# Joins of a block's half-words behind the sixth first-layer product, and token numbers behind a step's last copy

## The chip, the core and the metric

The kernel runs on one core of one Trainium2 chip. The metric is the device time of one execution in microseconds (us). A core has several engines that run side by side, each with its own queue of instructions, worked off in order: TensorE (PE in the profile; PEld is its weight load), VectorE (DVE), ScalarE (ACT), GpSimd (POOL) and SyncE (SP), which here only issues transfers (DMA). An instruction that waits holds up whatever stands behind it in its own queue.

## The reference

Two parts follow one another. First, attention over channels, for each of 4 batches with 5056 rows and 256 channels:

```python
qn = q / (np.linalg.norm(q, axis=1, keepdims=True) + 1e-06)
kn = k / (np.linalg.norm(k, axis=1, keepdims=True) + 1e-06)
s = kn.transpose(0, 2, 1) @ qn / tau      # 256 x 256 per batch
a = softmax(s)                            # over the last axis
x = v @ a                                 # 5056 x 256 per batch
```

Then a mixture of 8 experts over all 20224 tokens, in which each token goes to one expert:

```python
logits = x @ w_gate + modality_bias[modality_id]
e = argmax(logits);  gate = softmax(logits)[e]
out = gate * (relu(x @ w1[e]) @ w2[e])    # 256 -> 1024 -> 256
```

All of it is in 32-bit floating point.

## The kernel before

**Number format.** A 32-bit matrix product is written as three products of a faster format: each operand is split into a high part (a cast, on ACT) and a low part (the rest, a subtraction on DVE), and high by high, high by low and low by high are added up in PSUM. The splits of activations and weights are much of the work of ACT and DVE.

**Steps.** The tokens are handled in 40 steps of 512 (10 for each batch). A step loads its rows of v, transposes them, splits them (`vh`, `vl`), multiplies them by the batch's softmaxed matrix and the gate's weights (`av`, L574), and copies the result xp from PSUM into a tile x: for each of 4 groups of 128 tokens, ACT copies the high half-words (L580) and DVE the low ones. `route` (from L584) works out the softmax and the expert of each token (ACT's exponential ex is L592, the one-hot choice oh L600); `place` counts with small matmuls on PE (rp, L625 to L627) which row each token gets, writes the gate's denominator and the token's number into the two last columns of x (L646, on ACT), and sends the rows (`send`, POOL's indirect DMA, L469) to a buffer xs in DRAM that is sorted by expert. Three buffers serve x, two more at the start.

**The next batch's matrix.** Beside the steps of a batch run the pieces for the next batch's k-by-q matrix: loads of q and k, casts of them (L312), squares, and products g (L357). For the second batch, whose pieces run beside the first batch's steps, the casts and squares on ACT and DVE are ordered behind what an earlier step left in `routed`; its entry for ACT is the copy of the token numbers, L646.

**Blocks.** As soon as an expert has 512 rows, a block of them is chosen (`pick`) and put through the two layers; there are 40 blocks (the last two have 384 rows). Blocks 37 to 39 are chosen when all the steps are done and are called tail blocks. A block's pieces are:

- its loads on SP: the expert's weights, and its rows from xs by a transposing DMA into the tile Tx (L748, two buffers), which holds high and low half-words in separate planes;
- `tr_x`: for each of two halves `join` puts the half-words together to a 32-bit tile xt (high ones by ACT at L512, low ones by DVE at L513), which is then cast to xh (ACT, L808) and subtracted to xl (DVE, L809). xt shares three buffers with v's joins and with squares; xh and xl have two buffers each;
- `split_w(0)` to `split_w(3)`: casts of a quarter of both weights (ACT, L789) and their low parts (DVE, L796);
- `m1(j)`, eight first-layer products (PE, L823), each into one of two PSUM buffers hp, and its two evictions: hh = relu (ACT, L826) and hl, the low part (DVE, L827);
- `m2(j)`, the second-layer products (PE, L843), two products behind the first layer; the last two of a block run after the first product or two of the next block;
- `finish` and the stores (POOL, L469), each ordered behind a relu of the next block.

**What sets the order.** `block_stream` (L929) lists a block's pieces and puts those of the next block in between: `split_w(0)`, `tr_x` and `split_w(1)` at positions 7, 10 and 13 of the list, that is ahead of the fifth product, behind the sixth and ahead of the eighth; at 7, 14 and 15, behind the eighth product, if the next block is a tail block. The list begins with the block's first product, one second-layer product of the block before, and the second product; in a tail block the second-layer product comes first. The streams of a step, of a block and of the next batch are then interleaved. A planner decides from this program, from buffers and from its own simulated times in what order each engine's queue gets its instructions: an instruction that it takes to be ready early may come far ahead of its place in the program. `order` (L455) forbids that for one pair: the instruction doesn't come ahead of the other one. It adds no wait on the chip where both are on one engine.

Of the kernel before, what the change touches and what calls it, by code (L numbers as in the profile page):

```python
# [8 lines left out]
F32 = mybir.dt.float32  # L9
# [26 lines left out]
def kernel(  # L36
# [13 lines left out]
    nc = tc.nc  # L50
    P = 128
    B, N, C = q.shape
    T, D = out.shape
    E, _, FF = w1.shape
    TT = 4
# [5 lines left out]
    NJ = FF // P  # L61
# [40 lines left out]

    const.tile([P, 120], F32, name="filler0")
    ident = const.tile([P, P], F32, name="ident")
# [100 lines left out]
    turn = {}  # L205
# [302 lines left out]

    def join(dst, high, low):

        both = dst.bitcast(U16).rearrange("p (n w) -> p w n", w=2)
        nc.scalar.copy(both[:, 1, :], high)  # L512
        nc.vector.tensor_copy(both[:, 0, :], low)  # L513

    def va_pieces(b, s):
# [4 lines left out]
        st = {}  # L520
# [44 lines left out]
        def av(t):  # L565
# [13 lines left out]
            planes = st["x"][:, t, 0:D].bitcast(U16).rearrange("p (w n) -> p w n", w=2)  # L579
            nc.scalar.copy(planes[:, 0, :], halfwords[:, 1, :])  # L580
            copied[g, t] = nc.vector.tensor_copy(planes[:, 1, :], halfwords[:, 0, :]).ins
# [35 lines left out]
        def place():  # L617
# [22 lines left out]
            with nc.allow_low_precision("row numbers, below 2**24"):  # L640
                numbers = nc.vector.tensor_reduce(pi, pos.rearrange("p e t -> p t e"), AX.X, ALU.add)
            st["pi"] = pi
            routed[g] = [
                ("dve", numbers.ins),
                ("dve", nc.vector.reciprocal(x[:, :, D].bitcast(F32), sm).ins),
                ("act", nc.scalar.copy(x[:, :, D + 1], tokid[:, b, s * TT : (s + 1) * TT]).ins),  # L646
            ]
# [82 lines left out]
    def block_pieces(g, slot, picked, tail):  # L730
# [3 lines left out]
        rows = tt * P  # L734
        beside = {}

        banks = ["y0", "y1"] + (["g"] if slot == NB_MIN - 1 and tt == 3 else [])
# [40 lines left out]
        def split_w(ci):  # L778
            a, c = st["wr"][ci // 2]
            o = ci % 2  # L780
            if slot == 0 and ci == 0:
                p4.tile([P, 64], F32, tag="filler3", name="filler3", bufs=1)
            sa = a[:, :, o * FCH : (o + 1) * FCH]
# [15 lines left out]

        def tr_x():  # L800
            if slot == 0:
# [3 lines left out]
            for h in range(CH):  # L805
                vt = p3.tile([P, STEP], F32, tag="vt", name=f"xt_{slot}_{h}")
                join(vt[:, 0:rows], st["T"][:, 0, h, 0:rows], st["T"][:, 1, h, 0:rows])
                st["turned"] = nc.scalar.copy(xh[:, h, 0:rows], vt[:, 0:rows]).ins  # L808
                nc.vector.tensor_tensor(  # L809
                    xl[:, h, 0:rows], vt[:, 0:rows], xh[:, h, 0:rows].bitcast(F32), ALU.subtract  # L810
                )

        def m1(j):
# [8 lines left out]
            for i, (w, x, h) in enumerate(seq):  # L822
# [3 lines left out]
            relu = nc.scalar.activation(hh[:, 0:rows], hp[:, 0:rows], AF.Relu).ins  # L826
            nc.vector.scalar_tensor_tensor(  # L827
                hl[:, 0:rows], hp[:, 0:rows], 0.0, hh[:, 0:rows].bitcast(F32), ALU.max, ALU.subtract
            )
            st["h"][j] = (hh, hl)  # L830
            for f in beside.get(j, ()):
                f([relu])
# [58 lines left out]
        else:  # L891
# [4 lines left out]
            "slot": slot, "load": prep, "prep": prep2, "tail": tail, "first": lambda: m1(0), "body": body, "last": last,  # L896
            "stores": stores, "beside": beside,
        }
# [30 lines left out]
    def block_stream(blk, nxt):  # L929
# [4 lines left out]
        if nxt is not None:  # L934
            once(nxt, "load")
            done.add((nxt["slot"], "prep"))
            for o, f in reversed(list(zip((7, 14, 15) if nxt["tail"] else (7, 10, 13), nxt["prep"]))):
                body.insert(o, f)
# [4 lines left out]
        if not before:  # L943
            return [blk["first"]] + body
        if blk["tail"]:
            return [before[0], blk["first"], body[0]] + before[1:] + body[1:]
        return [blk["first"], before[0], body[0]] + before[1:] + body[1:]
# [141 lines left out]
```

## Time and profile before

| | us |
|---|---|
| median of 3 runs (lowest, highest) | 1219.19 (1216.51, 1222.01) |
| the profiled execution's own time | 1225.98 |
| its span | 1224.2 |
| PE busy | 1178.0 (96%) |
| DVE busy | 913.3 (75%) |
| ACT busy | 817.7 (67%) |
| POOL busy | 355.0 (29%) |

The profile is of one execution. A group's row reads: line, engine, operation, output <- inputs, count | busy us, mean ns of one | idle time ahead of it and what ended most of that. A timeline row reads: start in us, duration in us, engine, line, operation; in brackets the idle time ahead of it and what ended it. SPq is the issue of a transfer by SP. Matmuls are pipelined, so that the duration of one is longer than the distance to the next. A row of waits reads: engine, output, line <- engine, what was waited for, its line: sum in us, count, longest. PEclk is TensorE's granted clock as a share of full speed, "DMA share" the mean busy share of the core's 16 DMA engines.

### The profile page before, as it was taken

Reading aid. Unit: us, or ns where it says so; the run is one execution under the profiler, and the core shown is the slowest. Engines: PE = TensorE matmul, PEld = TensorE weight load, DVE = VectorE, ACT = ScalarE, POOL = GpSimd, SP = SyncE. Lnnn points to the kernel's source line nnn. Section 1 sums busy time; section 2 is a strip of 40 time slices with the busy share of each in tenths; the row PEclk is TensorE's granted clock in tenths of the full one; section 3 lists DMA queues with packets and bytes.
Section 4 is the critical chain, followed back from the end, with each engine's and each line's share of the span. In section 5 each row is a group of like instructions: output and inputs, shape, how many; then the busy total and the mean of one; then the engine's idle time right before and its main releaser. Section 6 shows DMA issues by size and latency. Waiting matters only on the chain. (4 is left out here: it accounts for less than half of the span.)

```text
span 1224.2 us, 23515 instructions
## 1 busy us (share of the span) xinstructions
PE 1178.0 (96%) x7780; PEld 1071.1 (87%) x7780; DVE 913.3 (75%) x2614; ACT 817.7 (67%) x1659; POOL 355.0 (29%) x345
## 2 busy tenths in 40 slices
PE   8987899999999999999999999999999999988997
PEld 7976799999999999989999999998888988887996
DVE  6787798898778888689887887676767666764552
ACT  6656677787777777588777776666666655544652
POOL 0053142322323222322333332222223322343121
PEclk9997899999999999999999999999999999998998
DMA  8989989499757787479777776647675655545320
GB/s 311 288 230 212 248 236 230 144 241 242 209 164 203 188 214 204 145 205 231 205 201 201 198 191 178 164 142 197 173 189 161 175 152 152 148 124 145 105 87 30
DMA packets 285844, 228.40 MB, mean 187 GB/s; under 512 B 185064, under 2 KB 243944, under 8 KB 285712
## 3 DMA queue, kind: packets, MB, share of 16 engines
q1 hardware_dynamic: 270032, 185.19, 58.2%
q0 software_dynamic: 15680, 41.61, 10.0%
q8 instruction: 63, 1.03, 0.4%
q14 instruction: 69, 0.57, 0.2%
HBM read 128.79 MB, written 43.43 MB: 141 GB/s over the span
## 5 line engine op out<-in xcount | busy, mean ns | idle before, releaser
L843 PE MATMUL y<-w2h,hh 128*128 128x256 f32 x1256 | 356.1, 284 | 0.0
L843 PE MATMUL y<-w2l,hh 128*128 128x256 f32 x1256 | 354.2, 282 | 0.0
L843 PE MATMUL y<-w2h,hl 128*128 128x256 f32 x1256 | 352.6, 281 | 0.1
L469 POOL DMA_INDIRECT xs<-x,pi x160 | 183.5, 1147 | 404.5 <-DVE pr L691 199.8
L469 POOL DMA_INDIRECT out_dram<-yo,gt x158 | 157.7, 998 | 428.3 <-ACT hh L826 251.0
L823 PE MATMUL hp<-xh,w1h 128*128 128x512 f32 (+1 forms) x640 | 254.5, 398 | 12.7 <-DVE hl L827 11.4
L823 PE MATMUL hp<-xh,w1l 128*128 128x512 f32 (+1 forms) x640 | 253.9, 397 | 0.0
L823 PE MATMUL hp<-xl,w1h 128*128 128x512 f32 (+1 forms) x640 | 252.1, 394 | 0.0
L843 PEld LDWEIGHTS y<-w2h,hh 128*128 128x128 f32 x1256 | 238.6, 190 | 12.7 <-issue 4.0
L843 PEld LDWEIGHTS y<-w2l,hh 128*128 128x128 f32 x1256 | 237.9, 189 | 8.0
L827 DVE SCALAR_TENSOR_TENSOR hl<-hp,hh 128x512 fp32r<-128x512 f32 (+1 forms) x320 | 217.1, 679 | 33.8 <-ACT hh L826 32.8
L843 PEld LDWEIGHTS y<-w2h,hl 128*128 128x128 f32 x1256 | 237.9, 189 | 0.3 <-DVE hl L827 0.3
L826 ACT ACTIVATE hh<-hp 128x512 fp32r<-128x512 f32 (+1 forms) x320 | 189.5, 592 | 50.9 <-PE hp L823 47.8
L789 ACT CAST w1h<-w1r 128x512 fp32r<-128x512 f32 x160 | 99.1, 619 | 110.0 <-PE hp L823 93.5
L796 DVE TENSOR_TENSOR w1l<-w1r,w1h 128x512 fp32r<-128x512 f32 x160 | 109.9, 687 | 52.8 <-ACT w1h L789 45.6
L823 PEld LDWEIGHTS hp<-xh,w1h 128*128 128x128 f32 x640 | 121.2, 190 | 29.7 <-DVE hl L827 13.3
L823 PEld LDWEIGHTS hp<-xh,w1l 128*128 128x128 f32 x640 | 121.3, 189 | 27.7
L796 DVE TENSOR_TENSOR w2l<-w2r,w2h 128x512 fp32r<-128x512 f32 x160 | 110.0, 687 | 45.7 <-ACT w2h L789 28.8
L823 PEld LDWEIGHTS hp<-xl,w1h 128*128 128x128 f32 x640 | 121.4, 190 | 15.1 <-DVE xl L809 0.2
L512 ACT COPY xt<-Tx 128x512 uint16<-128x512 uint16 (+1 forms) x80 | 61.7, 775 | 91.0 <-DMA Tx<-xs 87.3
L789 ACT CAST w2h<-w2r 128x512 fp32r<-128x512 f32 x160 | 100.0, 625 | 16.5 <-PE y L843 14.1
L513 DVE COPY xt<-Tx 128x512 uint16<-128x512 uint16 (+1 forms) x80 | 36.1, 460 | 80.5 <-DMA Tx<-xs 80.5
(160 smaller groups left out, 1910.0 us busy)
## 6 DMA issues: line engine op xcount, KB each, us to landing
w1r<-in_moe_w_dram SPq DMA_DIRECT2D x80, 512.0 KB
w2r<-in_moe_w_dram SPq DMA_DIRECT2D x80, 512.0 KB
q<-in_q_dram SPq DMA_DIRECT2D x35, 512.0 KB
k<-in_k_dram SPq DMA_DIRECT2D x35, 512.0 KB
pl<-T SPq DMA_DIRECT2D x120, 128.0 KB
v<-in_v_dram SPq DMA_DIRECT2D x6, 512.0 KB
xs<-x,pi POOLq DMA_INDIRECT x160
out_dram<-yo,gt POOLq DMA_INDIRECT x158
```

The lines of the kernel that those rows point to most:

```text
L469: ins = nc.gpsimd.indirect_dma_start(out=dst, out_offset=bass.IndirectOffsetOnAxis(ap=idx, axis=0), in_=rows, in_offset=None, bounds_check ...
L512: nc.scalar.copy(both[:, 1, :], high)
L513: nc.vector.tensor_copy(both[:, 0, :], low)
L789: ins = nc.scalar.copy(hi, src).ins
L796: nc.vector.tensor_tensor(lo, src, hi.bitcast(F32), ALU.subtract)
L823: nc.tensor.matmul(hp[:, 0:rows], w[:, h, fs], x[:, h, 0:rows], start=i == 0, stop=i == len(seq) - 1)
L826: relu = nc.scalar.activation(hh[:, 0:rows], hp[:, 0:rows], AF.Relu).ins
L827: nc.vector.scalar_tensor_tensor(hl[:, 0:rows], hp[:, 0:rows], 0.0, hh[:, 0:rows].bitcast(F32), ALU.max, ALU.subtract)
L843: ins = nc.tensor.matmul(y, a[:, tsl], w[:, j % 2, :], start=(j == 0 and i == 0 and t % per == 0), stop=(j == NJ - 1 and i == 2), skip_gro ...
```

## The change

1. The joins of a block (both halves, ACT's and DVE's) are ordered behind the evictions of the sixth first-layer product of the block before it: ACT's behind the relu, DVE's behind the low part. The first block's joins stay without such an order.
2. The copy of a step's token numbers is ordered behind the step's last ACT copy of x. As `routed` holds that copy, the second batch's casts and squares that are ordered behind it move along.
3. For tail blocks, the pieces of the next block stand at the same positions as elsewhere (7, 10, 13), and the block's list begins with its own first product as elsewhere.
4. Two tiles that only take up room change in size (120 to 104 and 64 to 72 floats in each partition), which shifts the addresses of the tiles behind them.

```diff
@@ -100,7 +100,7 @@
 
 
 
-    const.tile([P, 120], F32, name="filler0")
+    const.tile([P, 104], F32, name="filler0")
     ident = const.tile([P, P], F32, name="ident")
     make_identity(nc, ident)
     ones = const.tile([P, P], F32, name="ones")
@@ -506,11 +506,11 @@
                 nc.sync.dma_start(out[part * W : (part + 1) * W, w, :, 0:rows], T[w::2, part::2, 0:rows])
         return out
 
-    def join(dst, high, low):
+    def join(dst, high, low, behind=()):
 
         both = dst.bitcast(U16).rearrange("p (n w) -> p w n", w=2)
-        nc.scalar.copy(both[:, 1, :], high)
-        nc.vector.tensor_copy(both[:, 0, :], low)
+        order(nc.scalar.copy(both[:, 1, :], high).ins, behind[:1])
+        order(nc.vector.tensor_copy(both[:, 0, :], low).ins, behind[1:])
 
     def va_pieces(b, s):
         rows = min(STEP, N - s * STEP)
@@ -577,7 +577,7 @@
                 )
             halfwords = xp[:, 0:D].bitcast(U16).rearrange("p (n w) -> p w n", w=2)
             planes = st["x"][:, t, 0:D].bitcast(U16).rearrange("p (w n) -> p w n", w=2)
-            nc.scalar.copy(planes[:, 0, :], halfwords[:, 1, :])
+            st["out"] = nc.scalar.copy(planes[:, 0, :], halfwords[:, 1, :]).ins
             copied[g, t] = nc.vector.tensor_copy(planes[:, 1, :], halfwords[:, 0, :]).ins
             nc.vector.tensor_tensor(st["L"][:, t, :], xp[:, D:DE], bsel[b][:, s * TT + t, :], ALU.add)
 
@@ -640,10 +640,12 @@
             with nc.allow_low_precision("row numbers, below 2**24"):
                 numbers = nc.vector.tensor_reduce(pi, pos.rearrange("p e t -> p t e"), AX.X, ALU.add)
             st["pi"] = pi
+            named = nc.scalar.copy(x[:, :, D + 1], tokid[:, b, s * TT : (s + 1) * TT]).ins
+            order(named, [st["out"]])
             routed[g] = [
                 ("dve", numbers.ins),
                 ("dve", nc.vector.reciprocal(x[:, :, D].bitcast(F32), sm).ins),
-                ("act", nc.scalar.copy(x[:, :, D + 1], tokid[:, b, s * TT : (s + 1) * TT]).ins),
+                ("act", named),
             ]
             if g not in HELD:
                 send()
@@ -733,6 +735,7 @@
         tt = tiles(slot)
         rows = tt * P
         beside = {}
+        evicted = {}
 
         banks = ["y0", "y1"] + (["g"] if slot == NB_MIN - 1 and tt == 3 else [])
         per = -(-tt // len(banks))
@@ -779,7 +782,7 @@
             a, c = st["wr"][ci // 2]
             o = ci % 2
             if slot == 0 and ci == 0:
-                p4.tile([P, 64], F32, tag="filler3", name="filler3", bufs=1)
+                p4.tile([P, 72], F32, tag="filler3", name="filler3", bufs=1)
             sa = a[:, :, o * FCH : (o + 1) * FCH]
             sc = c[:, 2 * o : 2 * o + 2, :]
             res = []
@@ -797,14 +800,14 @@
                 res += [hi, lo]
             st["wc"][ci] = res
 
-        def tr_x():
+        def tr_x(behind=()):
             if slot == 0:
                 p2.tile([P, 24], F32, tag="filler4", name="filler4")
             xh = st["xh"] = p2.tile([P, CH, BLK], F32R, tag="xh", name=f"xh_{slot}")
             xl = st["xl"] = p2.tile([P, CH, BLK], F32R, tag="xl", name=f"xl_{slot}")
             for h in range(CH):
                 vt = p3.tile([P, STEP], F32, tag="vt", name=f"xt_{slot}_{h}")
-                join(vt[:, 0:rows], st["T"][:, 0, h, 0:rows], st["T"][:, 1, h, 0:rows])
+                join(vt[:, 0:rows], st["T"][:, 0, h, 0:rows], st["T"][:, 1, h, 0:rows], behind)
                 st["turned"] = nc.scalar.copy(xh[:, h, 0:rows], vt[:, 0:rows]).ins
                 nc.vector.tensor_tensor(
                     xl[:, h, 0:rows], vt[:, 0:rows], xh[:, h, 0:rows].bitcast(F32), ALU.subtract
@@ -824,10 +827,11 @@
             hh = p3.tile([P, BLK], F32R, tag="hh", name=f"hh_{slot}_{j}")
             hl = p3.tile([P, BLK], F32R, tag="hl", name=f"hl_{slot}_{j}")
             relu = nc.scalar.activation(hh[:, 0:rows], hp[:, 0:rows], AF.Relu).ins
-            nc.vector.scalar_tensor_tensor(
+            low = nc.vector.scalar_tensor_tensor(
                 hl[:, 0:rows], hp[:, 0:rows], 0.0, hh[:, 0:rows].bitcast(F32), ALU.max, ALU.subtract
-            )
+            ).ins
             st["h"][j] = (hh, hl)
+            evicted[j] = [relu, low]
             for f in beside.get(j, ()):
                 f([relu])
 
@@ -894,7 +898,7 @@
         stores = [] if slot >= NB_MIN - 1 else [lambda behind, t=t: store(t, behind) for t in range(tt)]
         return {
             "slot": slot, "load": prep, "prep": prep2, "tail": tail, "first": lambda: m1(0), "body": body, "last": last,
-            "stores": stores, "beside": beside,
+            "stores": stores, "beside": beside, "evicted": evicted,
         }
 
 
@@ -934,7 +938,8 @@
         if nxt is not None:
             once(nxt, "load")
             done.add((nxt["slot"], "prep"))
-            for o, f in reversed(list(zip((7, 14, 15) if nxt["tail"] else (7, 10, 13), nxt["prep"]))):
+            split0, turn, split1 = nxt["prep"]
+            for o, f in reversed(list(zip((7, 10, 13), (split0, lambda: turn(blk["evicted"][NJ - 3]), split1)))):
                 body.insert(o, f)
         before = open_blk[0]["last"] if open_blk[0] is not None else []
         for i, f in enumerate(open_blk[0]["stores"] if before else []):
@@ -942,8 +947,6 @@
         open_blk[0] = blk
         if not before:
             return [blk["first"]] + body
-        if blk["tail"]:
-            return [before[0], blk["first"], body[0]] + before[1:] + body[1:]
         return [blk["first"], before[0], body[0]] + before[1:] + body[1:]
 
     va = [va_pieces(*divmod(g, NS)) for g in range(G)]
```

## The prediction

> **What bounds the kernel now.** I read the page's head and groups first, then what the engines wait for, then busy time by stage.
>
> ```profile
> span 1224.2 us, 23515 instructions
> ...
> L843 PE MATMUL y<-w2h,hh 128*128 128x256 f32 x1256 | 356.1, 284 | 0.0
> ...
> L843 PE MATMUL y<-w2h,hl 128*128 128x256 f32 x1256 | 352.6, 281 | 0.1
> ...
> L789 ACT CAST w1h<-w1r 128x512 fp32r<-128x512 f32 x160 | 99.1, 619 | 110.0 <-PE hp L823 93.5
> ```
>
> The stages, cut at the gaps in TensorE's work; the first column after the stage is its length, the second PE's busy time:
>
> ```profile
> core 0: us, PE busy (x) PEld busy (x) DVE busy (x) ACT busy (x) POOL busy (x), PEclk, DMA share, GB/s
> ...
> 135.00:147.00 12.00, 8.02 (x37) 6.96 (x36) 6.24 (x27) 6.79 (x15) 0.98 (x1) 0.72 1.01 291
> 147.00:830.00 683.00, 681.82 (x4673) 624.35 (x4672) 562.62 (x1547) 508.03 (x1027) 208.78 (x193) 1.00 0.74 197
> 830.00:1075.70 245.70, 239.44 (x1582) 215.64 (x1581) 168.65 (x538) 150.16 (x309) 75.44 (x75) 1.00 0.62 169
> 1075.70:1103.30 27.60, 24.31 (x147) 21.85 (x146) 17.68 (x72) 11.20 (x22) 12.04 (x12) 0.94 0.48 126
> 1103.30:1133.30 30.00, 25.75 (x147) 22.77 (x146) 13.59 (x23) 14.62 (x28) 9.88 (x9) 0.89 0.49 136
> ...
> 1157.10:1179.60 22.50, 22.50 (x146) 20.33 (x145) 11.78 (x21) 11.63 (x23) 3.91 (x4) 1.00 0.38 117
> ```
>
> From 147 to 830 PE idles 683.00 − 681.82 = 1.2 us: that stretch is a queue of matmuls at full clock, and this change takes no matmul away. What can be won lies ahead of 147 and behind 830. The last three rows are blocks 34, 35 and 37, each of the same 146 to 147 matmuls: block 37, with no gap, takes 22.50, the other two 27.60 and 30.00. The waits say what stands behind the gaps; the columns are wait, count and longest:
>
> ```profile
> PE rp L625 <- DVE oh L600: 13.2, 3, 8.9
> PE hp L823 <- DVE hl L827: 11.4, 8, 3.8
> ...
> ACT xt L512 <- DMA Tx<-xs: 87.3, 25, 6.3
> ACT x L646 <- DMA xs<-x,pi: 7.7, 2, 6.7
> ```
>
> PE's 11.4 us are put down to DVE's evictions, but an eviction is 0.7 us of work. ACT stands 87.3 us in 25 waits of the join for a block's transposed rows Tx. What that does, in blocks 34 and 35:
>
> ```profile
> 1087.35 0.76 ACT L512 COPY xt<-Tx 128x512 uint16<-128x512 uint16 x1 [4.36 <-DMA Tx<-xs]
> 1087.99 0.58 ACT L826 ACTIVATE hh<-hp 128x512 fp32r<-128x512 f32 x1
> ...
> 1090.41 0.50 PE L823 MATMUL hp<-xh,w1h 128*128 128x512 f32 x1 [3.29 <-DVE hl L827]
> ...
> 1114.87 0.63 ACT L512 COPY xt<-Tx 128x384 uint16<-128x384 uint16 x1 [3.43 <-DMA Tx<-xs]
> ```
>
> The join stands in ACT's queue (its low half likewise in DVE's) until Tx has landed, the relu of a finished product behind it; both hp buffers stay full, and PE stops. The rows so awaited aren't even needed yet, as a block of the middle shows:
>
> ```profile
> 623.47 0.79 ACT L512 COPY xt<-Tx 128x512 uint16<-128x512 uint16 x1 [2.54 <-DMA Tx<-xs]
> ...
> 607.61 0.39 PE L823 MATMUL hp<-xh,w1h 128*128 128x512 f32 x1
> 636.07 0.39 PE L823 MATMUL hp<-xh,w1h 128*128 128x512 f32 x1
> 636.30 0.39 PE L823 MATMUL hp<-xl,w1h 128*128 128x512 f32 x1
> ...
> 636.79 0.68 DVE L809 TENSOR_TENSOR xl<-xt,xh 128x512 fp32r<-128x512 f32 x1
> ```
>
> Blocks begin 636.07 − 607.61 = 28.46 us apart. The join of 623.47 gets its xl at 636.79, after the block of 636.07 has read its own xl (636.30). So it belongs to the block after that, due near 664.5: joined 41 us ahead.
>
> **Part 1: joins behind the sixth product's evictions.** No instruction is added; the joins move most of a block later, when Tx has long landed, and evictions no longer stand behind the wait. *Tail.* Against block 37, blocks 34 and 35 lose 27.60 + 30.00 − 2 × 22.50 = 12.6 us: PE's idle time 3.29 + 4.25 = 7.5 (27.60 − 24.31 and 30.00 − 25.75), and about 5 of slower matmuls after each gap. The granted clock shows these, and one more stretch that part 2 needs:
>
> ```profile
> 139.30:146.10 6.80, 5.87 (x23) 5.07 (x23) 4.80 (x22) 4.38 (x9) 0.22 (x1) 0.50 1.00 334
> 1091.60:1095.00 3.40, 3.40 (x16) 3.23 (x15) 3.23 (x16) 0.60 (x1) 2.07 (x3) 0.50 0.76 227
> 1115.50:1122.30 6.80, 5.80 (x20) 5.13 (x21) 3.44 (x6) 1.84 (x4) 4.13 (x4) 0.50 0.34 106
> ```
>
> 3.40 and 6.80 us at clock 0.50 lose half of PE's busy time there, 1.7 + 2.9 = 4.6. I take 12; bounds 7.5 and 12.6. The Trainium skill, "TensorE: Matmul & The Clock Gate", section "Part 1: The HAM clock gate", says that the clock falls after a whole idle window of about 3.4 us and needs one busy window to come back; by it each gap would cost half of 3.4, together 3.4 instead of 4.6, and the total would come out 1.2 us later than mine. The rows agree for the first gap (3.40) and not for the second, twice as long.
>
> *830 to 1075.* PE idles 245.70 − 239.44 = 6.3 us. Of the 11.4 us in 8 hp waits above, 3.3 and 3.8 were the tail's; the other six, 4.3 together, are of the same make, nearly all here:
>
> ```profile
> 906.60 0.78 ACT L512 COPY xt<-Tx 128x512 uint16<-128x512 uint16 x1 [4.05 <-DMA Tx<-xs]
> ```
>
> I take these 4; bounds 0 (another queue member stands there instead) and 6.3.
>
> *What the delay costs.* After the sixth product's relu come two joins (0.78 each), two casts (0.62 each, as the weights' of one shape) and the last xl (0.68): 0.59 + 1.56 + 1.24 + 0.68 ≈ 4.1 us if nothing comes between.
>
> ```profile
> 655.65 0.59 ACT L826 ACTIVATE hh<-hp 128x512 fp32r<-128x512 f32 x1
> 664.54 0.39 PE L823 MATMUL hp<-xh,w1h 128*128 128x512 f32 x1
> ...
> 655.65:664.54 8.89, 8.89 (x68) 8.16 (x66) 8.07 (x27) 7.51 (x16) 0.98 (x1) 1.00 0.74 175
> ...
> 1149.20 0.59 ACT L826 ACTIVATE hh<-hp 128x512 fp32r<-128x512 f32 x1
> ...
> 1157.14 0.39 PE L823 MATMUL hp<-xh,w1h 128*128 128x512 f32 x1
> ```
>
> In the middle there are 8.89 us for it, margin 4.7; ACT is already busy for 7.51 of them, some of it casts of weights and of a later block that can wait. At the tail's end 7.94, which the old order there had put one product (a sixteenth of 22.50, 1.4 us) later; margin about 2.4. I take 0; bounds 0 and rival B. Tx has two buffers, so the load of the block after next now waits for these joins on SP; its rows are joined a whole block later, which covers the 6.3 us that a join waited at most. Behind it on SP stand the v transposes and the next weights; that is the cover to watch.
>
> *Tail order.* Turning at the usual place and one first-layer product first: 0, since it changes the order of the same matmuls; with late joins it would cost 1.4.
>
> **Part 2: token numbers behind the step's last copy.** No instruction is added; L646 moves past copies on ACT's queue.
>
> ```profile
> 94.81 0.20 ACT L646 COPY x<-tokid 128x4 int32<-128x4 int32 x1 [6.68 <-DMA xs<-x,pi]
> 98.15 0.18 PE L625 MATMUL rp<-oh,trim 128*128 128x32 bf16 x1 [8.90 <-DVE oh L600]
> 99.85 0.77 ACT L512 COPY xt<-Tx 128x512 uint16<-128x512 uint16 x1
> 107.00 0.73 PE L823 MATMUL hp<-xh,w1h 128*128 128x512 f32 x2 [1.03 <-ACT x L580]
> ...
> 137.46 1.14 ACT L312 CAST qs<-q 128x512 fp32r<-128x512 f32 x2 [4.11 <-DMA q<-in_q_dram]
> ...
> 159.34 0.36 ACT L580 COPY x<-xp 128x256 uint16<-128x256 uint16 x1
> 171.93 1.59 PE L357 MATMUL g<-qs,ks 128*128 128x256 f32 x12
> ```
>
> At 94.81 the copy has held ACT for 6.68 us until scatters of its x buffer were done; the softmax of the step stood behind it, and PE 8.90. With copies ahead of it, these go on. But the first block's rows are only joined at 99.85, after their own transfer, so its first product comes at about 102 at best, 5 us earlier. At 137.46 the q casts, which hang on the same list of routed work, wait for q; they go behind step 7's last copy, 159.34, which frees ACT. Their products run at 171.93, a cover of 12 us. This could save the stage's 12.00 − 8.02 = 4.0 us of idle time and half of PE's 5.87 busy at clock 0.50, 2.9; together with the first, at most 12. At the other end a q wait of 4.11 merely comes elsewhere: −4. The middle of −4 and 12 is 4, and I take it: the first stage is short of transfers too (DMA share 1.01 from 135 to 147), so not the full gain.
>
> **Part 3: fillers.** The addresses of later tiles shift. The nearest rows are the two second-layer groups of equal shape: 356.1 and 352.6 us. I take 0, bounds ±3.5.
>
> **Sum.** 12 + 4 + 4 = 20. The profiled execution takes 1225.98 (the span and 1.8 around it), which is 6.8 above the median of 1219.19; against itself it would come to 1206. If that is waiting for transfers, some of my 20 is missing in the median run; I can't tell, keep 20 there, and get **1199**.
>
> **Rivals.** *A: only the tail gains.* At the start transfers set the pace, and the short gaps of 830 to 1075 reappear at other members of ACT's queue. For: DMA share 1.01, and 8.9 us of rp waits that need q and the scatters anyway. Against: the gaps have one and the same releaser. 1219.2 − 12 = 1207.
> *B: slower, the joins come too late.* The first product of each block waits for its last xl. It decides once more than 4.7 us of other ACT work comes between relu and last cast: one split of the weights is four casts of 0.62, 2.5 us, and two of them 5.0. For: ACT has 7.51 busy in 8.89. Against: three of these are the joins and casts that move. At 1.5 us in each of 683 / 28.46 = 24 blocks it costs 36: 1199 + 36 = 1235.
> *C: the wait moves.* The join still waits for Tx, since Tx's own load now stands behind later joins on SP, with the v transposes behind it; evictions seven and eight stand behind it as before. For: ACT's 87.3 us of these waits show that loads land late against the queue. Against: loads now have a block's time. Gains and new gaps cancel: 1217.
> *That the order is not what it says*: it only forbids earlier joins, so the planner may put them later still; that is B's mechanism.
>
> **From this the numbers.** Forecast 0.60 (its own range 1188 to 1208, 12.6 + 6.3 + 12 saved at one end, the tail's 7.5 and half of the other 8 at the other), A 0.18, C 0.10, B 0.12. A measurement here tells about 0.5% from no change, 6.1 us: faster is below 1213.1, slower above 1225.3. The forecast and A are faster, 0.78 and a little of C, 0.79; C gives 0.10 for the same; B 0.11 with its near end within the bound. Range 1187 to 1217: it takes in A and C and leaves B and the far tails out.
>
> **What would show it.** Right: blocks 34 and 35 last 22.5 to 23.5 us, no clock of 0.50 after 1080, and the joins' 87.3 us of waiting fall below 20. Rows 830 to 1075 show PE idle below 2.5 us. The wait of L646 for scatters falls below 2 and the first block's first product comes before 104. The middle stage remains 683 within 3. Wrong: waits of first-layer products for xl (B), of joins for Tx (C), or rp waits that stay near 13 (A).

## The result and the profile after

The changed kernel takes 1203.80 us (median of 4 runs, 1203.36 to 1206.59) against 1218.18 (median of 4, 1216.51 to 1222.01): ratio 0.988, 95% interval 0.985 to 0.991, or 14.4 us. The forecast was 1199, or 20 us. The two profiled executions lie further apart, 1225.98 and 1203.36, 22.6 us, because the one before was 7.8 us above its median and the one after is 0.4 below.

The head and one matmul group of the page of the changed kernel (its lines stand 3 or 4 further down than before: L826 was L823, L847 was L843, L811 was L808, L829 was L826, L751 was L748, and the token copy L646 is now L643):

```profile
span 1201.6 us, 23565 instructions
...
PE 1170.8 (97%) x7780; PEld 1069.3 (89%) x7780; DVE 914.6 (76%) x2614; ACT 808.5 (67%) x1659; POOL 381.2 (32%) x345
...
L826 PE MATMUL hp<-xh,w1h 128*128 128x512 f32 (+1 forms) x640 | 251.2, 393 | 0.6 <-ACT xh L811 0.6
```

What PE and then ACT wait for (sum, count, longest):

```profile
PE rp L625 <- DVE sm L614: 6.3, 4, 3.4
PE g L357 <- ACT ks L312: 4.5, 1, 4.5
PE g L357 <- DMA k<-in_k_dram: 4.4, 1, 4.4
PE rp L626 <- DVE run L611: 3.0, 2, 2.4
...
PE hp L826 <- ACT xh L811: 0.6, 1, 0.6
...
ACT x L580 <- DMA xs<-x,pi: 9.3, 6, 1.6
...
ACT acc L336 <- DMA k<-in_k_dram: 5.5, 2, 4.5
...
ACT xt L512 <- DMA Tx<-xs: 5.2, 1, 5.2
```

The joins' 87.3 us of waiting are 5.2, and PE's 11.4 us of hp waits behind DVE's evictions are gone. So is ACT's wait in the token copy; copies of x now wait for scatters instead (9.3 us in 6 waits, the longest 1.6). PE's waits are for routing (rp) and for the next batch's products (g). By stage, cut at first-layer products of blocks 0, 2, 12, 14, 24, 34 and 37:

```profile
core 0: us, PE busy (x) PEld busy (x) DVE busy (x) ACT busy (x) POOL busy (x), PEclk, DMA share, GB/s
107.38:158.87 51.49, 51.31 (x325) 45.59 (x326) 45.27 (x130) 36.52 (x73) 12.93 (x12) 0.97 1.02 261
158.87:454.01 295.14, 294.44 (x2025) 270.41 (x2023) 246.38 (x671) 221.64 (x455) 100.90 (x80) 1.00 0.72 202
454.01:516.38 62.37, 59.79 (x393) 54.71 (x392) 45.56 (x130) 39.82 (x82) 18.63 (x16) 0.95 0.65 182
516.38:805.67 289.29, 288.68 (x1977) 264.79 (x1975) 233.57 (x657) 208.08 (x427) 96.65 (x82) 1.00 0.67 193
805.67:1066.09 260.42, 259.70 (x1737) 236.21 (x1735) 189.45 (x582) 168.80 (x349) 85.28 (x81) 1.00 0.64 172
1066.09:1132.97 66.88, 66.88 (x435) 60.81 (x433) 44.36 (x121) 38.13 (x72) 27.67 (x26) 1.00 0.53 147
```

The last row is blocks 34 to 36 with no gap, 22.29 us each. The rows to compare with are those of the first experiment, which has the same addresses and the old order.

### The profile page after: what moved, and what is told of

Read it like the earlier page. It is cut to its first block, busy times and chain, and to the rows that moved or that the text cites. A ratio compares the mean times of both kernels' runs of the same rounds, so it can differ in the third digit from the quotient of the medians.

```text
span 1201.6 us, 23565 instructions
## 1 busy us (share of the span) xinstructions
PE 1170.8 (97%) x7780; PEld 1069.3 (89%) x7780; DVE 914.6 (76%) x2614; ACT 808.5 (67%) x1659; POOL 381.2 (32%) x345
## 3 DMA queue, kind: packets, MB, share of 16 engines
q1 hardware_dynamic: 270032, 185.19, 56.9%
## 4 chain that ended last, share of the span: by engine, by line
PE 71%; DVE 13%; issue 8%; ACT 4%; DMA 2%; POOL 2%; SPq 0%; POOLq 0%; ACTq 0%; DVEq 0%
PE hp L826 27%; PE y L847 26%; PE g L357 8%; PE xp L574 8%; DVE xl L812 3%; DVE hl L830 2%; POOL out_dram L469 1%; DVE vt L513 1%; ACT xt L512 1%; DVE acc L338 1%; DVE vl L561 1%; DVE xt L513 1%; DVE w1l L799 1%; ACT w1h L792 1%; DVE x L581 1%
## 5 line engine op out<-in xcount | busy, mean ns | idle before, releaser
L847 PE MATMUL y<-w2h,hh 128*128 128x256 f32 x1256 | 355.8, 283 | 0.0
L847 PE MATMUL y<-w2l,hh 128*128 128x256 f32 x1256 | 352.5, 281 | 0.0
L847 PE MATMUL y<-w2h,hl 128*128 128x256 f32 x1256 | 351.2, 280 | 0.1
L469 POOL DMA_INDIRECT xs<-x,pi x160 | 195.8, 1224 | 425.1 <-ACT hh L829 213.7
L469 POOL DMA_INDIRECT out_dram<-yo,gt x158 | 171.3, 1084 | 362.6 <-ACT hh L829 245.3
L826 PE MATMUL hp<-xh,w1h 128*128 128x512 f32 (+1 forms) x640 | 251.2, 393 | 0.6 <-ACT xh L811 0.6
L826 PE MATMUL hp<-xl,w1h 128*128 128x512 f32 (+1 forms) x640 | 251.6, 393 | 0.0
L826 PE MATMUL hp<-xh,w1l 128*128 128x512 f32 (+1 forms) x640 | 249.4, 390 | 0.0
L847 PEld LDWEIGHTS y<-w2h,hh 128*128 128x128 f32 x1256 | 237.4, 189 | 8.7 <-ACT hh L829 0.2
L847 PEld LDWEIGHTS y<-w2l,hh 128*128 128x128 f32 x1256 | 237.2, 189 | 7.6
L847 PEld LDWEIGHTS y<-w2h,hl 128*128 128x128 f32 x1256 | 236.1, 188 | 0.3 <-DVE hl L830 0.3
L829 ACT ACTIVATE hh<-hp 128x512 fp32r<-128x512 f32 (+1 forms) x320 | 189.2, 591 | 62.5 <-PE hp L826 62.5
L826 PEld LDWEIGHTS hp<-xh,w1l 128*128 128x128 f32 x640 | 120.8, 189 | 26.2
L826 PEld LDWEIGHTS hp<-xh,w1h 128*128 128x128 f32 x640 | 120.8, 189 | 14.7 <-ACT xh L811 0.9
L826 PEld LDWEIGHTS hp<-xl,w1h 128*128 128x128 f32 x640 | 120.9, 189 | 13.2
L580 ACT COPY x<-xp 128x256 uint16<-128x256 uint16 x160 | 59.0, 372 | 60.8 <-PE xp L574 44.1
L581 DVE COPY x<-xp 128x256 uint16<-128x256 uint16 x160 | 67.1, 420 | 38.3 <-ACT x L580 37.4
```

Source lines behind the costliest of these rows:

```text
L469: ins = nc.gpsimd.indirect_dma_start(out=dst, out_offset=bass.IndirectOffsetOnAxis(ap=idx, axis=0), in_=rows, in_offset=None, bounds_check ...
L580: st["out"] = nc.scalar.copy(planes[:, 0, :], halfwords[:, 1, :]).ins
L826: nc.tensor.matmul(hp[:, 0:rows], w[:, h, fs], x[:, h, 0:rows], start=i == 0, stop=i == len(seq) - 1)
L847: ins = nc.tensor.matmul(y, a[:, tsl], w[:, j % 2, :], start=(j == 0 and i == 0 and t % per == 0), stop=(j == NJ - 1 and i == 2), skip_gro ...
```

## The experiments

All ratios are to the kernel before, with 95% intervals; they differ from the quotient of the two medians beside them by up to 0.0011. Runs of one group were made on one chip, each group with its own runs of the kernel before. Group one: the first four; group two: the next four; group three: the third product and the late square; group four: the fourth product, alone and with the late square.

**1. Addresses alone.**

```diff
-    const.tile([P, 120], F32, name="filler0")
+    const.tile([P, 104], F32, name="filler0")
...
-                p4.tile([P, 64], F32, tag="filler3", name="filler3", bufs=1)
+                p4.tile([P, 72], F32, tag="filler3", name="filler3", bufs=1)
```

> Only the two room-taking tiles change in size (120 to 104 and 64 to 72 floats); every engine's order of instructions is that of the kernel before. Theory of the prediction: addresses cost nothing, 1218 within 3.5. Rival, from the two traces: the matmuls themselves became faster through the addresses. In undisturbed stretches first-layer matmuls followed each other at 233.6 ns before and at 231.2 after; over 1920 of these that is 4.6 us, and the three second-layer groups fell by 3.4 us together: 8 us, 1210, with the tail's and the start's gaps still there.

Measured: 1219.13 against 1224.29, ratio 0.9964 (0.9945 to 0.9982). By the ratio it is 4.4 us faster (by the two medians 5.2), between the two expectations and clear of zero. The page shows matmuls of both layers shorter, with the same instructions in the same order on every engine (first-layer 398 ns before, 395 here; second-layer 281 before, 279 here). The first of the rows is that of the kernel before:

```profile
L823 PE MATMUL hp<-xh,w1h 128*128 128x512 f32 (+1 forms) x640 | 254.5, 398 | 12.7 <-DVE hl L827 11.4
...
L843 PE MATMUL y<-w2h,hl 128*128 128x256 f32 x1256 | 350.6, 279 | 0.1
L823 PE MATMUL hp<-xh,w1h 128*128 128x512 f32 (+1 forms) x640 | 252.8, 395 | 14.5 <-DVE hl L827 13.6
```

Its stages, cut at the same products as those of the changed kernel:

```profile
107.69:167.69 60.00, 54.25 (x326) 47.91 (x326) 46.91 (x136) 39.71 (x78) 12.13 (x12) 0.91 1.05 240
167.69:460.46 292.77, 292.65 (x2025) 269.32 (x2023) 250.16 (x676) 225.95 (x455) 93.71 (x80) 1.00 0.76 207
460.46:517.13 56.67, 56.67 (x392) 52.14 (x391) 41.41 (x120) 36.10 (x74) 17.11 (x16) 1.00 0.63 186
517.13:805.45 288.32, 287.06 (x1977) 263.46 (x1975) 234.86 (x657) 212.59 (x427) 84.53 (x82) 1.00 0.71 193
805.45:1072.09 266.64, 261.05 (x1737) 236.01 (x1736) 187.91 (x590) 170.35 (x351) 83.64 (x82) 1.00 0.61 168
1072.09:1152.13 80.04, 72.06 (x447) 64.74 (x446) 44.87 (x118) 39.68 (x77) 26.17 (x25) 0.96 0.46 128
```

So the new order alone changed, stage by stage: start 51.49 − 60.00 = −8.5, middle +2.4, blocks 12 and 13 +5.7, then +1.0, late stage −6.2, tail −13.2. The three stages between the start and 805 lose 9.0 us together, a little more than the start gains. These are two single executions of different groups; experiment 8 shows which of the terms come again.

**2. Token numbers alone.**

```diff
-            nc.scalar.copy(planes[:, 0, :], halfwords[:, 1, :])
+            st["out"] = nc.scalar.copy(planes[:, 0, :], halfwords[:, 1, :]).ins
...
+            order(named, [st["out"]])
```

> Only the copy of the token numbers is ordered behind the step's last copy of x. Theory: the casts of q wait no longer ahead of the second block, so the stall of PE at 136 and the half clock behind it are gone, 7.4 us; the first block's start stays (107.4 after against 107.0 before); the tail's gaps stay. 1218 - 7 = 1211. Rival: that stall went because the joins moved and the whole plan with them; then this alone gives 0 to 3, 1215 to 1218, with the wait of the q casts still at 4.

Measured: 1229.83 against 1224.29, ratio 1.0047 (1.0029 to 1.0065): slower by 5.5 us. Both expectations miss.

**3. Joins and tail positions alone.**

```diff
+        order(nc.scalar.copy(both[:, 1, :], high).ins, behind[:1])
+        order(nc.vector.tensor_copy(both[:, 0, :], low).ins, behind[1:])
...
+            for o, f in reversed(list(zip((7, 10, 13), (split0, lambda: turn(blk["evicted"][NJ - 3]), split1)))):
```

> Only the joins' order, with the tail blocks at the common positions and in the common order. Theory: the joins' waits for transposed rows fall from 87 us to under 20, blocks 34 and 35 take 22.5 us (13 us saved of the profiled execution), and from 830 to 1076 PE idles under 1.5 us (5 to 8 saved); nothing at the start. The profiled execution before was 8 above the median, so 1218 - 13 = 1205 if that surplus lay in these very waits, 1198 if not. Rival, that the common order of the tail's list and not the joins freed the evictions: the tail gets its gain, the stretch from 830 keeps its 6 us of gaps, 1207.

Measured: 1214.40, ratio 0.9925 (0.9901 to 0.9950): 9.2 us faster by the ratio, 9.9 by the medians. The tail does as the theory says (blocks 34 to 36 take 67.36 us together, 22.45 each), but the total gain is less than either expectation.

**4. Both, with the old addresses.** The change without the edit of experiment 1.

> The whole change but for the two tiles' sizes; the engines' orders are those of the changed kernel. Theory that addresses cost nothing: 1204 as the changed kernel. Rival that they give 8 us: 1212, with first-layer matmuls at 233 to 234 ns from one to the next instead of 231.

Measured: 1212.19, ratio 0.9912 (0.9887 to 0.9936). With the new addresses the ratio is 0.988; the intervals overlap, so these times alone don't show that addresses are worth some of the gain. The traces do: a tail block without a gap takes 22.45 us here and 22.29 with the new addresses.

The start, from block 0 to block 2, of experiments 2, 3 and 4 in this order:

```profile
106.29:163.00 56.71, 52.63 (x325) 45.68 (x326) 46.76 (x138) 38.99 (x79) 12.57 (x12) 0.97 1.04 236
105.41:165.38 59.97, 54.52 (x326) 48.42 (x326) 46.20 (x134) 38.60 (x76) 13.52 (x13) 0.91 0.99 236
108.13:160.35 52.22, 52.10 (x325) 46.32 (x326) 45.39 (x130) 36.49 (x73) 12.56 (x12) 0.95 1.05 259
```

Before, the same stretch is 166.31 − 107.00 = 59.3. The token numbers alone save 2.6 of it, the joins alone nothing, both 7.1. What stalls each single part there, first in experiment 2 (ACT, then PE), then in experiment 3:

```profile
149.94 0.76 ACT L512 COPY vt<-pl 128x512 uint16<-128x512 uint16 x1 [4.79 <-DMA pl<-T]
...
151.93 0.50 PE L825 MATMUL hp<-xh,w1h 128*128 128x512 f32 x1 [1.81 <-DVE hl L829]
```

```profile
138.86 0.18 PE L625 MATMUL rp<-oh,trim 128*128 128x32 bf16 x1 [4.93 <-DVE oh L600]
```

With the token numbers alone the wait of the q casts is gone, but a join waits ahead of an eviction: it is one of v's (`vt`), not a block's, and PE loses 1.81 us behind it. With the joins alone the q casts still wait (5.1 us on ACT, 4.93 at PE). With both, neither wait is there. Why v's transposed rows come late in experiment 2 was not followed up. Between joins alone and joins with token numbers the totals, 0.9925 and 0.9912, can't be told apart.

**5. The tail's positions and list order alone.**

```diff
-            for o, f in reversed(list(zip((7, 14, 15) if nxt["tail"] else (7, 10, 13), nxt["prep"]))):
+            for o, f in reversed(list(zip((7, 10, 13), nxt["prep"]))):
...
-        if blk["tail"]:
-            return [before[0], blk["first"], body[0]] + before[1:] + body[1:]
```

> Of the change only the tail blocks' common positions and list order; joins as before, addresses as before. Theory: the joins still stand ahead of the evictions and wait for transposed rows, so blocks 34 and 35 keep about 27 and 30 us and the joins' 80 us of waits stay; only the 1.4 us shift between the third and the last blocks goes: ratio 1.000, 1219 on the prediction's scale. Rival, that the tail's gain came from the positions: blocks 34 to 36 at 22.5, 12 us faster, 1206.

Measured: 1221.48 against 1220.74, ratio 1.0006 (0.9991 to 1.0020). Blocks 34, 35 and 36 of it:

```profile
1073.37:1099.07 25.70, 22.78 (x146) 20.41 (x145) 17.54 (x72) 11.19 (x22) 11.05 (x12) 1.00 0.41 118
1099.07:1129.51 30.44, 24.54 (x147) 21.65 (x146) 13.47 (x23) 14.62 (x28) 10.27 (x10) 0.94 0.55 148
1129.51:1151.96 22.45, 22.45 (x147) 20.29 (x145) 12.24 (x21) 12.50 (x26) 3.92 (x4) 1.00 0.37 117
```

Two gaps stay; block 36 loses its 1.4 us, which come back from block 37 on (67.06 us from its first product to the end before, 68.47 here), so that the total gains nothing. The tail's gain is the joins'.

**6. Joins behind the eighth product.** Their place in the list moves behind that product too, and behind `split_w(1)`.

```diff
-zip((7, 10, 13), (split0, lambda: turn(blk["evicted"][NJ - 3]), split1))
+zip((7, 13, 14), (split0, split1, lambda: turn(blk["evicted"][NJ - 1])))
```

> The changed kernel with the joins behind the eighth product's evictions instead of the sixth's (and turned behind that product in the list). In the changed kernel xl is complete 5.2 us ahead of the next block's first product in the middle and 2.2 ahead in the tail; the eighth eviction ends 8.0 us (5.6 in the tail) later than the sixth. Theory (the margin is real, rival B of the prediction decides past 4.7): every block's first product waits for its xl, 3.5 us each, or 0.7 if the plan puts the two second-layer products of 1.4 ahead of it; 38 blocks: 27 to 130 us slower than the changed kernel, 1230 to 1335. Rival, that the margin doesn't matter since products have other work before them: 1204 to 1208.

Measured: 1213.18, ratio 0.9940 (0.9918 to 0.9962); the changed kernel beside it 1206.71. 6.5 us slower, far less than the theory's 27 at least. PE's wait of that kind, and one instance in the tail:

```profile
PE hp L826 <- ACT xh L811: 6.4, 30, 0.6
```

```profile
1120.30 0.73 PE L826 MATMUL hp<-xh,w1h 128*128 128x512 f32 x2 [0.25 <-ACT xh L811]
```

The waits exist, in 30 places, but each is 0.2 on average: in the instance above, second-layer products of the old block run right up to the new block's first one (the last starts at 1119.77). The margin is real; a block that misses it pays much less than the 0.7 to 3.5 us expected.

**7. The counting products in another order.**

```diff
-            nc.tensor.matmul(rp[:, 0:W], trim, ohf, start=True, stop=False, skip_group_check=True)
-            nc.tensor.matmul(rp[:, 0:W], onesb, rtf, start=False, stop=True, skip_group_check=True)
+            nc.tensor.matmul(rp[:, 0:W], onesb, rtf, start=True, stop=False, skip_group_check=True)
...
+            nc.tensor.matmul(rp[:, 0:W], trim, ohf, start=False, stop=True, skip_group_check=True)
```

> The changed kernel with the three small counting products in another order: the two that need the running counts first, the one that needs only the one-hot choice last. In the profile before, the three ran as one group in the middle steps; in the changed kernel the first runs alone and the other two later, behind six to twelve second-layer matmuls, and a block of the middle takes 28.63 us where the kernel with the same addresses and old order takes 28.32. Theory: this second change between the two kinds of matmul costs the 0.2 to 0.3 us; joined again, 20 to 28 middle blocks give back 4 to 8 us: 1197 to 1200, 28.35 us for a block. Rival, that the 0.3 us is something else of the new order: 1204.

What led to it: the products of one step in experiment 1, and in the changed kernel, which puts second-layer products between the first and the second.

```profile
690.54 0.19 PE L625 MATMUL rp<-oh,trim 128*128 128x32 bf16 x1
690.58 0.18 PE L626 MATMUL rp<-run,onesb 128*128 128x32 bf16 x1
```

```profile
689.65 0.19 PE L625 MATMUL rp<-oh,trim 128*128 128x32 bf16 x1
...
690.36 0.18 PE L626 MATMUL rp<-run,onesb 128*128 128x32 bf16 x1
```

Measured: 1207.86, ratio 0.9899 (0.9879 to 0.9918), no gain over the 1206.71 beside it. The theory of a switch between kinds of matmul falls. Standing together, the three show what they cost, in PE's waits of this experiment:

```profile
PE rp L625 <- DVE run L611: 15.2, 23, 4.6
```

They wait for the routing's running counts in 23 steps; two steps ahead of block 2 have 7.4 of the 15.2 us, and a step of the middle typically 0.2. In the changed kernel the same lateness is hidden between the products. When the counts (`run`, on DVE) of the step shown above were worked out, first in experiment 1, then in the changed kernel:

```profile
689.63 0.23 DVE L611 TENSOR_TENSOR_SCAN run<-keep,oh 128x32 bf16<-128x32 bf16 x1
```

```profile
690.08 0.22 DVE L611 TENSOR_TENSOR_SCAN run<-keep,oh 128x32 bf16<-128x32 bf16 x1
```

There they end at 689.86, 0.7 us ahead of their product; here at 690.30, 0.06 ahead, so the product starts as soon as they are there. So it is in all but one of the 18 steps beside blocks 5 to 22 of the changed kernel (0.05 to 0.15 us); in experiment 1 most of them have 0.7 to 1.6 us to spare.

**8. The changed kernel again.** No edit.

> The changed kernel itself, on the same chip as the others of this call: 1204, ratio 0.988 to the kernel before. It gives the yardstick for the other three.

Measured: 1206.71, ratio 0.9887 (0.9868 to 0.9906): the first result again. The lengths of its stages, in us, beside those of the other executions, cut at the same products (experiment 5 has the old joins and addresses and is of the same group as this one):

| blocks | before | 1 | 5 | changed | changed again |
|---|---|---|---|---|---|
| 0 and 1 | 59.3 | 60.0 | 58.1 | 51.5 | 52.1 |
| 2 to 11 | 294.1 | 292.8 | 294.1 | 295.1 | 295.1 |
| 12 and 13 | 56.9 | 56.7 | 56.9 | 62.4 | 61.0 |
| 14 to 23 | 289.6 | 288.3 | 289.6 | 289.3 | 290.7 |
| 24 to 33 | 268.9 | 266.6 | 268.1 | 260.4 | 262.8 |
| 34 to 36 | 81.4 | 80.0 | 78.6 | 66.9 | 66.9 |

Against experiment 1 the repetition gains 7.9 at the start, loses 9.0 from block 2 to 23 as the first execution did, and gains 13.2 in the tail; but from block 24 to 33 it gains 3.9, not 6.2.

**9. Joins behind the third product.**

```diff
-turn(blk["evicted"][NJ - 3])
+turn(blk["evicted"][2])
```

> The changed kernel with the joins behind the third product's evictions instead of the sixth's. The counting products of a step wait for the running counts in 23 steps when they stand together (15.2 us, in the kernel with the counts first), and a middle block takes 28.63 us instead of 28.34 with the same addresses. Theory A: the joins, two casts and low parts now crowd ACT and DVE just where the step's routing has to go through; three products earlier they stand clear of it, a middle block takes 28.35 again, 5 us less over some 18 blocks, and the tail keeps its 22.3: ratio 0.983 to 0.985. Theory B: any place within the same block crowds the routing: 28.6 and ratio 0.988. If the early place makes the joins wait for their rows again, the joins' waits for rows rise above 20 us.

Measured: 1201.26, ratio 0.9834 (0.9813 to 0.9855): theory A, and faster than the changed kernel. Its stages from block 2 to 12, 12 to 14 and 24 to 34, and a wait of PE:

```profile
160.71:453.70 292.99, 292.93 (x2024) 269.50 (x2023) 251.24 (x671) 220.90 (x452) 96.02 (x80) 1.00 0.77 207
453.70:510.48 56.78, 56.78 (x393) 52.22 (x391) 42.85 (x123) 38.55 (x78) 17.56 (x16) 1.00 0.67 184
...
799.66:1064.21 264.55, 260.19 (x1736) 235.15 (x1735) 192.00 (x588) 167.77 (x349) 87.61 (x82) 1.00 0.62 170
```

```profile
PE y L847 <- ACT yo L861: 3.5, 7, 1.0
```

292.99 and 56.78 are those of experiment 1 within 0.2: the loss of the middle is gone. (The planner's order of other instructions follows the joins; only their place was edited.) The late stage, 264.55, is longer than in the two executions of the changed kernel, 260.42 and 262.75. Second-layer products there wait for the finishing copies, 3.2 us of the 3.5; that this is all of the difference isn't shown.

**10. First squares of the third and fourth batch later.**

```diff
-(lambda: routed.get(g, routed[g - 1])) if b == 0 and g > 0 else (),
+(lambda: routed.get(g, routed[g - 1])) if b == 0 and g > 0 or i == 0 and b > 0 else (),
```

> The changed kernel with the first pieces of the third and fourth batch (casts and squares on ACT and DVE) ordered behind the last routed step, as the second batch's pieces are already. In the changed kernel blocks 12 and 13 take 31.7 to 32.5 and 29.3 to 29.9 us, before 28.47 each: at 470.8 ACT waits 4.5 us for k in the first square, the load of k having stood on SP behind a block's row load that waited 5.3 us for scatters; routing comes late and PE waits 2.75 us, then half clock. Theory: this wait is the whole loss there; with the square later blocks 12 and 13 take 28.6 to 28.7 each, 4 us less, ratio 0.985. Rival: another wait takes its place, the routing is late there for the joins' sake: blocks 12 and 13 stay over 60 together, 0.988.

What led to it, in the changed kernel's timeline of SP, ACT and PE:

```profile
467.92 1.94 SPq L751 DMA_TRANSPOSE Tx<-xs  x1
...
470.52 0.47 SPq L296 DMA_DIRECT2D k<-in_k_dram  x1
...
475.29 0.63 ACT L336 ACTIVATE acc<-k 128x512 f32<-128x512 f32 x1 [4.51 <-DMA k<-in_k_dram]
...
483.49 0.21 PE L625 MATMUL rp<-oh,trim 128*128 128x32 bf16 x1 [2.58 <-DVE sm L614]
```

Measured: 1200.84, ratio 0.9832 (0.9814 to 0.9850). Blocks 12 and 13:

```profile
456.26:513.92 57.66, 57.23 (x393) 52.40 (x392) 43.44 (x126) 39.50 (x82) 18.97 (x16) 1.00 0.75 196
```

57.66 instead of 62.37 (60.95 in the repetition): the theory holds, most of the loss there is the square that waits for k. In the changed kernel the load of k had been issued at 470.52, behind the issue of a block's rows; before, one was issued at 459.55, ahead of the rows at 471.06.

**11 and 12. Joins behind the fourth product; that with the later squares.** The edits of 9 (with 3 in place of 2) and of 10.

> The changed kernel with the joins behind the fourth product's evictions; beside the third (ratio 0.983) and the sixth (0.988) it shows whether the gain grows with distance from the step's routing. Behind the third product middle blocks take 28.30 to 28.49 us with no loss in blocks 12 and 13, but the stretch from block 25 to 33 has waits of second-layer matmuls for the finishing copies, 3.5 us, which the sixth has not. Theory: a place between has the gain of the middle (28.3 to 28.4) and loses less than 3.5 behind block 25: 1197 to 1200 on the scale of 1220 before, 0.981 to 0.983. Rival: the routing is already crowded at the fourth: 28.6 for a middle block, 0.986 to 0.988.

> The fourth product together with the later first squares of the third and fourth batch. Behind the sixth product these gave 5 us, most of it in blocks 12 and 13; behind the third these blocks are at 28.30 and 28.47 without them. Theory: nothing is left for them to save, within 0.15% of the fourth product alone. Rival: they save 2 to 4 us elsewhere (start of the fourth batch, around block 24, 29.5 to 30.1 us there): 0.979 to 0.981.

Measured: 1201.41, ratio 0.9828 (0.9800 to 0.9856), and 1198.72 against 1223.39, ratio 0.9809 (0.9780 to 0.9838). Third, fourth, and sixth with later squares can't be told apart; nor can the last two be told from each other, so whether anything was left for the squares to save stays open. The last kernel, faster than the changed one (0.9868 to 0.9906 in its repetition), has the smallest ratio of all.

## Why the prediction was right, and where not

**The tail: right.** Blocks 34 and 35 were to fall to 22.5; they take 22.3. Against the same addresses the three blocks give 13.2, of which experiment 5 puts about 1.4 to the list order, given back at the end: 11.8 for the forecast 12. Experiments 3 and 5 show that the joins' order does it, and that the two gaps stay without it.

**830 to 1075: right in kind, its size open within 4 to 6.** 4 was taken of at most 6.3; 6.2 came in the first execution, 3.9 in the repetition. In the first, nearly all of PE's gaps there went (260.42 − 259.70 = 0.7 us are left), those of the rp waits too, of which nothing had been counted; in the repetition 2.75 are left, in other waits. The working's six waits were not "nearly all here": 3.3 of their 4.3 us lie in this stretch.

**The middle at 0: wrong.** This is the mis-sized term: 9.0 us were lost from block 2 to block 24 (2.37 + 5.70 + 0.97), in the repetition 9.0 again; the working's sign, the middle unchanged within 3, failed (against the kernel before itself these stages are 6.2 longer). Rival B had the right worry, late joins on crowded engines, but the wrong victim. Not the next block's xl was late (PE waits 0.6 us in all for xh); the routing of the step was: the running counts are done just ahead of their product, 0.05 to 0.15 us, where it had mostly been 0.7 to 1.6. Experiment 9, in which only the place of the joins was edited, brings back both the 2.4 and the 5.7, and the counts then have mostly 0.7 to 1.7 us to spare (0.36 in experiment 11, behind the fourth product). Experiment 10 shows that the 5.7 need two things: the joins' plan, in which a k load is issued behind a row load, and the square that waits for it on ACT. That SP's queue was the cover to watch had been said, though with v's transposes and weights as what would be late, not k. That the crowd on ACT or that on DVE is the one that counts was not separated. Rival B's price, lateness times blocks, fell too: experiment 6 lost 6.5 us, not 27 or more. (The working's margin of 4.7 comes out at 4.8.)

**The start at 4: mis-sized, and half of its working wrong.** The first block was to start at 102; it starts at 107.38. ACT's one long wait for scatters did go, and PE's 8.90 us of rp wait became 3.4 at most, but PE then stands for the next batch's products, in the changed kernel's timeline:

```profile
104.45 0.58 PE L357 MATMUL g<-qs,ks 128*128 128x256 f32 x1 [4.46 <-ACT ks L312]
```

This is rival A's mechanism, in that one place. The second half came in full, 8.5 us from block 0 to 2 against at most 6.9 in the working (7.9 in the repetition; 5.9 between experiments 5 and 8, of one group). But experiments 2 and 3 show that it isn't the token numbers' alone, as part 2 had it: alone these save 2.6 there and cost 5.5 in total. Their trace has a loss from block 2 to 12, 297.13 us against 294.05 before; its cause was not followed up.

**Addresses at 0, bounds 3.5: wrong by 4.4** (2.2 to 6.7 by the interval). The row used for the bounds was of second-layer groups only; the first-layer products gained as well.

**The sum on the median: wrong, and covered by luck.** Terms by the first traces: 11.8 + 6.2 + 8.5 − 9.0 + 4.4 = 21.9, near the 22.6 between the two profiled executions. That it is also near the forecast 20 is luck: the start and the addresses brought more than forecast, and the loss of the middle, put at nothing, took about as much away. The medians gained 14.4. The step that failed is that all of it was kept against the median. The profiled execution before was 7.8 us above its median, and this surplus is about what is missing. The prediction had named that as a possibility without a number.

Where the 7.8 us lay can be seen in part: the profiled execution of experiment 5 is 3.8 us shorter, and the table of experiment 8 has 1.2 of these at the start, 0.8 from block 24 to 33, and 1.4 in the gaps of the tail (2.8 less the 1.4 of the list order), the stretches that the change was to shorten. The rest is open. A surplus of this size is also what lies between groups: the median of the kernel before was 1218.18 beside the result and 1224.29 in group one, from which the row of experiment 1 is. Within group two, where both are of one chip, experiments 5 and 8 differ by 16.7 us in their profiled executions and by 14.8 in their medians.

## What to carry to other kernels

An instruction that waits for a transfer belongs in an engine's queue behind the work that others need, but moving it late makes it part of the crowd at its new place: after such a move, look at every other chain that goes through the same engine, not only at the consumer of the moved work. Try two or three places: here the third and fourth product beat the sixth, and the eighth lost 6.5 us, nearly half of the gain. And set a sum of stalls against the profiled execution first; if that one lies above the median, take the excess off before naming a time.

## What the runs showed of the hardware

The granted clock did not go by the length of PE's gap alone. In the changed kernel a gap of 2.5 us went with 6.8 us at about half clock, from 0.6 us before its end on; in experiment 5 a longer one, 2.9 us, had full clock in all of the 12 us around it:

```profile
480.90:483.40 2.50, 0.02 (x1) 0.00 (x0) 2.50 (x12) 2.50 (x7) 0.00 (x0) 0.91 0.39 102
482.80:489.60 6.80, 6.11 (x24) 5.44 (x25) 5.33 (x19) 5.22 (x11) 0.61 (x1) 0.51 0.56 159
```

```profile
1084.90:1087.80 2.90, 0.12 (x1) 0.12 (x2) 2.80 (x15) 2.90 (x6) 1.47 (x2) 1.00 0.02 3
1084.00:1096.00 12.00, 9.08 (x59) 8.06 (x58) 10.68 (x49) 6.12 (x11) 6.87 (x7) 1.00 0.38 121
```

The Trainium skill, "TensorE: Matmul & The Clock Gate", section "Part 1: The HAM clock gate", has the clock fall after a whole idle window of about 3.4 us. The trace disagrees for the first gap, which is shorter and still followed by half clock, and doesn't contradict it for the second.

The other surprise is the matmuls' dependence on where their tiles lie: 4.4 us from 64 and 32 bytes of shift, with all instructions and their order the same. Which operand's address counts was not tried.
